# Three quarters of w_out loaded ahead of batch 1, the first batch's second layer cut 12 to 4, 36 fillers in small groups: one change to a fused attention and MoE kernel on one core

## The chip, the core and the metric

The kernel runs on one core of one Trainium2 chip. Five engines work side by side, each through its own queue in program order: PE (TensorE, matrix products and transposes), ACT (ScalarE), DVE (VectorE), POOL (GpSimd) and SP (SyncE, here only an issuer of transfers). Transfers between HBM and on-chip memory run on 16 DMA engines; SP's and ACT's go through hardware queues, POOL's through a software queue. The metric is the device time of one execution in microseconds.

## The reference

Eight batches of linear attention with cosine weights, heads concatenated, feed a two-layer network whose gate is h cos(h).

```python
def phi(x, c, s):
    r = np.maximum(x, 0.0)
    return np.concatenate([r * c, r * s], axis=-1)
q_p = phi(q, cos_w, sin_w)
k_p = phi(k, cos_w, sin_w)
kv = np.einsum('bhsf,bhsd->bhfd', k_p, v)
z = np.sum(k_p, axis=2)
num = np.einsum('bhsf,bhfd->bhsd', q_p, kv)
den = np.einsum('bhsf,bhf->bhs', q_p, z)[..., None] + 1e-06
...
h = x @ w_in
g = h * np.cos(h)
return (g @ w_out).astype(np.float32)
```

q, k and v are 8 x 8 heads x 576 tokens x 64, in 32-bit floats; x has 4608 tokens of 512; w_in is 512 x 2048, w_out 2048 x 512.

## The kernel before

**Stages.** Tokens go through in chunks of 512: chunk b holds most of batch b, cut into four tiles of 128 tokens, and a fifth tile of each pair of batches gathers the rest for a ninth chunk. For each batch: `load` brings q, k and v to the raw buffers (one buffer per name, reused by every batch; two transfers each, one for each half of the partitions); `prep` (L364 to L369) multiplies max(x, 0) with a cosine or sine and rounds to 16 bits, once for each tile and each of the two functions g, on ACT or DVE; `cast_v` rounds V; `q_pe` (L428, copies at L435 and L437) transposes a tile of q on PE; `kv` (L397) sums k times v over all tiles, in two halves of four heads (copied out at L410 and L412, or L415); `num` (L464, then L481 to L485 on DVE) forms numerators and denominators of a tile and divides; `x_pe` (L519, L524) transposes the result. `layer1` (L575 for chunks 0 and 1) multiplies with w_in, and `gate` takes the cosine on ACT (L547) and the product on DVE (L549). `layer2_plain` (L878), for chunk 0 alone, multiplies with w_out; from chunk 1 on a form with sums of blocks is used (`layer2`, L953; the sums over w_out are made once on DVE, `w_out_sums`, L901).

**Order.** The program records about 1,400 steps in `Plan`. A step may have several engines to choose from. Two literal tables, `STARTS` and `ENGS`, give each step a number and an engine; `run` sorts the steps by that number and emits them, so the table is the order on each engine's queue. The numbers in it have no other use.

**The front.** PE starts with matmuls on a constant tile, here called fillers (`warm`, L1041): 28 ahead of q's transposes, 17 after the first of these, and 4, 3 and 2 between the numerators of batch 0. Their results aren't used.

**Weights.** They come through POOL's queue in quarters, and are held back by small copies on POOL that write one element of each quarter's destination, so that the transfer has to come after them. `weights` lets w_in's first half go when a given piece of q has been prepared (`HQ` = tile, function, number of hops: the copy reads it through as many small copies); `weights2` lets the second half go when a tile of V has been cast (`WS2`), then w_out's first `WQ` quarters when w_in's first has landed. `hold_raw` (L1098) does the same for batch 1's raw buffers: they wait for the quarter that `RAW1` names. `part_of_w_out` (L1115) lets the rest of w_out go when a piece of batch 1's q has landed. `layer2_plain` sums over hidden units in two parts, and the first takes as many of the sixteen blocks of 128 as `WQ` quarters hold; the first part's result is copied out by ACT (L886), the second's added by DVE (L889):

```python
WQ = OPT["WQ"] * NJT // 4
for jh, js in enumerate((range(WQ), range(WQ, NJT))):
    for n, t in enumerate(range(NT)):
```

```python
GATE1 = ((w_in_sb[0:2, 0, R1 * Dff // 4 + 1:R1 * Dff // 4 + 2], [("w_in", R1)]) if R1 < 4 else
         (w_out_sb[0:2, (R1 - 4) * NJT // 4, 1:2], [("w_out", R1 - 4)]))
```

Of the kernel before, what the change touches and what calls it, by code (L numbers as in the profile page):

```python
# [13 lines left out]
F16 = mybir.dt.float16  # L14
# [3 lines left out]
OPT = dict(F16=0, WS2=[3, 1], HQ=[1, 0, 1], AQ=0, W2F=0, WQ=2, L2F=0, WFI=None, XPE=[0, 1, 2, 3, 4], FAST1={3:  # L18
           2, 4: 2, 5: 2, 6: 4, 7: 4, 8: 4}, MODE={}, HH='', LD=[['k', 0], ['v', 0], ['q', 0], ['k', 1], ['v',
           1], ['q', 1]], NB=[['A0', 'A1'], ['A0', 'A1', 'M0']], XB=[['B3'], ['B3', 'M1']], W0=5, W1=6,  # L20
           WF=[[2, 2, 2, 2], [2, 2, 0, 0]], HOLD=['k', 1], P0=0, RAW1=2, WO2=1, H1=0, DA=0, W2=0, SQ=0, NUZ=1)
# [1440 lines left out]
```

## Time and profile before

| | |
|---|---|
| device time, median of 3 runs | 281.50 us (281.26 to 281.94) |
| the profiled execution | 281.42 us, span 279.6 us |
| granted clock of PE | 1.00 |
| HBM read, written | 36.75 MB, 11.80 MB |

The span runs from the first to the last recorded instruction; 1.8 us of the execution's time lie around it. Rows of the timeline give start and length in us, engine, line, operation and what is written from what; in brackets stands the idle time before, and what ended it. The chain of waits is followed back from the last instruction; its rows are start, length, engine, tile and line. Rows of transfers end with the median time from issue to landing, and rows of DMA queues give packets, MB and share of the 16 engines' time.

### The profile page before, as it was taken

Reading aid. Unit: us, or ns where it says so; the run is one execution under the profiler, and the core shown is the slowest. Engines: PE = TensorE matmul, PEld = TensorE weight load, DVE = VectorE, ACT = ScalarE, POOL = GpSimd, SP = SyncE. Lnnn points to the kernel's source line nnn. Section 1 sums busy time; section 2 is a strip of 40 time slices with the busy share of each in tenths; the row PEclk is TensorE's granted clock in tenths of the full one; section 3 lists DMA queues with packets and bytes.
Section 4 is the critical chain, followed back from the end, with each engine's and each line's share of the span. In section 5 each row is a group of like instructions: output and inputs, shape, how many; then the busy total and the mean of one; then the engine's idle time right before and its main releaser. Section 6 shows DMA issues by size and latency. Waiting matters only on the chain.

```text
span 279.6 us, 6829 instructions
## 1 busy us (share of the span) xinstructions
PE 272.5 (97%) x2698; PEld 215.5 (77%) x2698; DVE 236.4 (85%) x442; ACT 210.0 (75%) x363; POOL 83.4 (30%) x104
## 2 busy tenths in 40 slices
PE   8999999999999999999999999999999999999993
PEld 2567867787966677769776878789988888888882
DVE  1767698989999999999999998989989879873952
ACT  2756699879998897788989978995758696776330
POOL 1340020030502101520440045132534372399210
PEclk9999999999999999999999999999999999999999
DMA  6999999989999999969999998739756495697125
GB/s 209 337 205 205 361 218 258 338 282 181 324 303 263 242 230 264 285 200 287 216 249 265 212 260 283 109 104 142 161 76 146 102 159 102 150 146 123 75 77 150
DMA packets 80223, 58.03 MB, mean 208 GB/s; under 512 B 43200, under 2 KB 77248, under 8 KB 80192
## 3 DMA queue, kind: packets, MB, share of 16 engines
q1 hardware_dynamic: 68960, 39.99, 59.3%
q0 software_dynamic: 10496, 17.04, 29.3%
q10 hardware_dynamic: 736, 0.57, 0.7%
q8 instruction: 21, 0.34, 0.5%
q14 instruction: 10, 0.08, 0.1%
HBM read 36.75 MB, written 11.80 MB: 174 GB/s over the span
## 4 chain that ended last, share of the span: by engine, by line
PE 92%; ACT 3%; DVE 2%; issue 1%; POOL 0%; ACTq 0%; POOLq 0%
PE M L953 34%; PE M L736 14%; PE M L608 11%; PE M L575 9%; PE TR L736 6%; PE ATT L1041 5%; PE ATT L464 3%; PE M L878 3%; PE ATT L397 3%; PE TR L608 2%; ACT KQ L368 1%; DVE XN L485 1%; PE M L428 1%; ACT V L382 0%; ACT ch L547 0%
## 5 line engine op out<-in xcount | busy, mean ns | idle before, releaser
L953 PEld LDWEIGHTS <-gT 128*128 128x128 f16 x560 | 53.9, 98 | 8.3
L953 PE MATMUL M<-w_out_sb,gT 128*128 128x256 f16 x448 | 57.1, 273 | 0.0
L549 DVE TENSOR_TENSOR gT<-M,ch 128x512 f16<-128x512 f32 x73 | 48.5, 684 | 5.9 <-ACT ch L547 5.7
L547 ACT ACTIVATE ch<-M 128x512 f32<-128x512 f32 x75 | 43.4, 596 | 12.2 <-PE M L575 5.4
L368 ACT ACTIVATE KQ<-km,CS 128x512 f16<-128x512 f32 x57 | 38.5, 718 | 1.6 <-DMA km<-in_k_dram 1.6
L964 ACT ACTIVATE ost<-M 128x512 f32<-128x512 f32 x41 | 24.3, 596 | 18.0 <-PE M L953 13.0
L368 ACT ACTIVATE KQ<-qm,CS 128x512 f16<-128x512 f32 x46 | 31.5, 721 | 4.0 <-DMA qm<-in_q_dram 4.0
L608 PE MATMUL M<-xT,w_in_sb 128*128 128x512 f16 x136 | 33.8, 379 | 0.0
L953 PE MATMUL M<-T,S 128*128 128x256 f16 x256 | 32.3, 273 | 0.0
L384 POOL CAST V<-vm 128x1024 f16<-128x1024 f32 (+1 forms) x18 | 15.8, 904 | 51.6 <-DVE den L481 21.6
L736 PEld LDWEIGHTS <-w_in_sb 128*128 128x128 f16 x288 | 27.3, 98 | 4.8 <-issue 0.3
L575 PE MATMUL M<-xT,w_in_sb 128*128 128x256 f16 x256 | 30.3, 273 | 0.3 <-DVE gT L549 0.3
L953 PEld LDWEIGHTS <-S 128*128 128x128 f16 x256 | 24.8, 98 | 4.1 <-DVE S L929 0.2
L575 PEld LDWEIGHTS <-w_in_sb 128*128 128x128 f16 x256 | 24.4, 98 | 3.9 <-issue 0.5
L748 DVE TENSOR_TENSOR Z<-M,Z 128x512 f32<-128x512 f32 x31 | 21.1, 687 | 4.3 <-PE M L736 3.2
L608 PEld LDWEIGHTS <-w_in_sb 128*128 128x128 f16 x160 | 14.9, 98 | 12.2
L549 POOL TENSOR_TENSOR gT<-Z,ch 128x512 f16<-128x512 f32 x5 | 6.3, 1268 | 56.6 <-ACT ch L547 20.0
L485 DVE TENSOR_TENSOR XN<-ATT,rec 128x512 f16<-128x512 f32 x32 | 22.1, 692 | 1.1
L464 PEld LDWEIGHTS <-qT 128*128 128x128 f16 (+1 forms) x320 | 14.8, 101 | 5.6 <-issue 3.5
L759 ACT ACTIVATE ch<-Z 128x1024 f32<-128x1024 f32 x12 | 12.7, 1057 | 6.9 <-DVE Z L748 4.9
L744 ACT ACTIVATE Z<-M 128x512 f32<-128x512 f32 x26 | 15.2, 596 | 3.4 <-PE M L736 2.4
L464 PE MATMUL ATT<-kvz,qT 128*128 128x65 f16 (+1 forms) x288 | 16.0, 195 | 0.8 <-DVE XN L485 0.5
(152 smaller groups left out, 519.3 us busy)
## 6 DMA issues: line engine op xcount, KB each, us to landing
out_dram<-ost POOLq DMA_DIRECT2D x38, 256.0 KB, 4.1
qm<-in_q_dram SPq DMA_DIRECT2D x8, 640.0 KB, 6.3
km<-in_k_dram SPq DMA_DIRECT2D x8, 640.0 KB, 7.1
qm<-in_q_dram SPq DMA_DIRECT2D x8, 512.0 KB, 5.7
km<-in_k_dram SPq DMA_DIRECT2D x8, 512.0 KB, 5.9
vm<-in_v_dram SPq DMA_DIRECT2D x6, 640.0 KB, 6.0
vm<-in_v_dram SPq DMA_DIRECT2D x6, 512.0 KB, 4.4
w_in_sb<-in_moe_w_in_dram POOLq DMA_DIRECT2D x4, 512.0 KB, 7.5
```

The lines of the kernel that those rows point to most:

```text
L368: fn = {"ACT": lambda: nc.scalar.activation(out=out_, in_=in_, func=AF.Relu, scale=sc), "DVE": lambda: nc.vector.tensor_scalar(out=out_, i ...
L384: "POOL": lambda: nc.gpsimd.tensor_copy(out=out_, in_=in_)}
L464: nc.tensor.matmul(bank[hb][ps, hh * D1:(hh + 1) * D1], lhsT=x[:, h, :], rhs=z[:, h, :], start=True, stop=True)
L485: nc.vector.tensor_tensor(out=split(x16[n][:, hs, :], k), in0=A[:, :, :, 0:D], in1=split(rec[n][:, hs], k).unsqueeze(3).broadcast_to((P, k ...
L547: act(0.5, due, lambda: nc.scalar.activation(out=ch[c], in_=bank, func=AF.Sin, bias=math.pi / 2.0, scale=1.0), [key], [("ch", c)])
L549: mul(due, 0.61, lambda q: q.tensor_tensor(out=dst, in0=bank if len(dst.shape) == 2 else bank.rearrange("p (j s) -> p j s", j=dst.shape[1] ...
L575: nc.tensor.matmul(M1[m][:, jj * 2 * P:(jj + 1) * 2 * P], lhsT=w_in_sb[:, cc, j * P:(j + 1) * P], rhs=X[:, cc, ts], start=(cc == 0), stop= ...
L608: nc.tensor.matmul(M, lhsT=w_in_sb[:, cc, j * P:(j + 1) * P], rhs=X[:, cc, :], start=(cc == 0), stop=(cc == NCT - 1))
L736: nc.tensor.matmul(bank[0][:, j * TH:(j + 1) * TH], lhsT=a(cc, j), rhs=b[:, cc, :], start=(first and j == 0 and cc == 0), stop=(last and j ...
L748: dve(0.61, due + 0.3, lambda: nc.vector.tensor_tensor(out=dst, in0=bank[0], in1=dst, op=ALU.add), [bank[1], key], [key])
L953: nc.tensor.matmul(bank[0][:, tt * MH:(tt + 1) * MH], lhsT=a[:, j, tt * P:(tt + 1) * P], rhs=b[:, j, :], start=(first and (apart or tt == ...
L964: act(0.5, due, lambda: nc.scalar.activation(out=dst, in_=view(bank), func=AF.Copy), [bank[1]], dk)
```

## The change

- `WQ` from 2 to 3: three quarters of w_out are asked for ahead of batch 1, one after; the first part of chunk 0's second layer sums 12 blocks, the second 4.
- `RAW1` from 2 to 4: batch 1's raw buffers wait for w_out's first quarter in place of w_in's third.
- `W2F` from 0 to 2: the release of w_out's last quarter reads a single element of q's first part, through one more small copy.
- `HQ` from tile 1 to tile 3: w_in's first half is let go by another tile of q.
- `FW`, new: the fillers ahead of batch 0's kv are 20, 4, 4, 4 and 4 (36) in place of 28 and 17 (45), as steps of their own, so that the table can put other steps between them.
- The tables are new. On PE they put the transposes of q's tiles 1, 0 and 3 after the first 20 fillers, then 4 fillers, tile 2's transposes, 12 fillers and kv; the copies of tiles 0 and 1 come ahead of k's preparations on DVE and ACT; batch 0's numerators begin with tile 0. For batch 1, three groups of 12 matmuls with w_out stand ahead of its first transposes, and DVE's first sum over w_out stands ahead of its norms. Batch 2's preparations of k are spread among batch 1's copies. One preparation of batch 2's k, one of batch 3's k and one of batch 3's q go from DVE to ACT. From about the second chunk's second layer on the order is the same on PE.

```diff
-OPT = dict(F16=0, WS2=[3, 1], HQ=[1, 0, 1], AQ=0, W2F=0, WQ=2, L2F=0, WFI=None, XPE=[0, 1, 2, 3, 4], FAST1={3:
...
+OPT = dict(F16=0, WS2=[3, 1], HQ=[3, 0, 1], AQ=0, FW=[20, 4, 4, 4, 4], W2F=2, WQ=3, L2F=0, WFI=None, XPE=[0,
...
-           WF=[[2, 2, 2, 2], [2, 2, 0, 0]], HOLD=['k', 1], P0=0, RAW1=2, WO2=1, H1=0, DA=0, W2=0, SQ=0, NUZ=1)
+           'M1']], W0=5, W1=6, WF=[[2, 2, 2, 2], [2, 2, 0, 0]], HOLD=['k', 1], P0=0, RAW1=4, WO2=1, H1=0,
+           DA=0, W2=0, SQ=0, NUZ=1)
...
-        warm(28, 9.05)
+        if OPT["FW"]:
+            for i, n in enumerate(OPT["FW"]):
+                warm(n, 7.5 if i == 0 else 0.2157 * n)
+        else:
+            warm(28, 9.05)
...
-        warm(17, 3.67, rd=[("TR", 0)])
+        if not OPT["FW"]:
+            warm(17, 3.67, rd=[("TR", 0)])
```

The rest of the diff is the tables.

More of the change, by code (lines that the diff above doesn't have):

```diff
@@ L15 @@
 SYNC = mybir.DependencyInfo(mybir.DependencyClass.Sync, mybir.DependencyReason.DATA)
-OPT = dict(F16=0, WS2=[3, 1], HQ=[1, 0, 1], AQ=0, W2F=0, WQ=2, L2F=0, WFI=None, XPE=[0, 1, 2, 3, 4], FAST1={3:
-           2, 4: 2, 5: 2, 6: 4, 7: 4, 8: 4}, MODE={}, HH='', LD=[['k', 0], ['v', 0], ['q', 0], ['k', 1], ['v',
-           1], ['q', 1]], NB=[['A0', 'A1'], ['A0', 'A1', 'M0']], XB=[['B3'], ['B3', 'M1']], W0=5, W1=6,
-           WF=[[2, 2, 2, 2], [2, 2, 0, 0]], HOLD=['k', 1], P0=0, RAW1=2, WO2=1, H1=0, DA=0, W2=0, SQ=0, NUZ=1)
@@ L24 @@
-STARTS = (
[98 rows of a table removed]
+OPT = dict(F16=0, WS2=[3, 1], HQ=[3, 0, 1], AQ=0, FW=[20, 4, 4, 4, 4], W2F=2, WQ=3, L2F=0, WFI=None, XPE=[0,
+           1, 2, 3, 4], FAST1={3: 2, 4: 2, 5: 2, 6: 4, 7: 4, 8: 4}, MODE={}, HH='', LD=[['k', 0], ['v', 0],
+           ['q', 0], ['k', 1], ['v', 1], ['q', 1]], NB=[['A0', 'A1'], ['A0', 'A1', 'M0']], XB=[['B3'], ['B3',
+           'M1']], W0=5, W1=6, WF=[[2, 2, 2, 2], [2, 2, 0, 0]], HOLD=['k', 1], P0=0, RAW1=4, WO2=1, H1=0,
+           DA=0, W2=0, SQ=0, NUZ=1)
+STARTS = (
[98 rows of a table added]
 )
@@ L124 @@
 ENGS = (
-    "DDPSSSSSSSSDAPDDDPADAPDDAPAGGGGPDADADDDADADADADDADADGGGGGGPPADPPDPPAPPDPPAPPDPPAPPDPAPAD"
-    "PADPADPADPADPADPADPADPADPADPADPADPADPADPADPADGSSGSSGGGGGSSSSDADADADADADAPDDAPADAPDDAPADA"
-    "DADADDADADPPAPPDPAPPDPAPPDPAPPDPAPDPPDPAPAPAPAPAPDPDGGPDPDGGPADPADPADPADPADPADPADPADPADP"
-    "ADPADPADPADPADPADPADDDDDSSSSSSADADAADDAAGGGPPADASDDSAASAASPPDPAPPDPAPPDPAPPDPADDDPPAPPDD"
-    "PPAPPAPPDPPDGGPPAGGPADPADPADPADPADPADPADPADPADPADPADPADPADPADPADPADSSSSSSDDAAAAAAAAGGGPP"
-    "ADASAASDASAASADPPDSPPDSPPDSPPDSSPPDSDDDDDDDPPAPPDDPPAPPAPPDPPDGGPPAGGDDDDPAPDAGPAPAPDPDA"
@@ L131 @@
-    "DPADPADPADPADPADPAPDAGPAPAPDPDADPADPADPADPADPADSSSSSSAAAAAADAAAGGGPPAAASAASAASADSPPDSPPD"
-    "SPPDSPPDSDDDPPAPPDDPPAPPAPPDPPDGGPPAGGDDDDPAPDAGPAPAPDPDADPADPADPADPADPADPAPDADPAPAPDPDA"
-    "DPADPADPADPADPADSSSSSSDDAAAAAAADGGGPPAADSAASDDSAASAAPPDSPPDSPPDSPPDSSPPDSDDDPPAPPADPPAGG"
-    "PPAPPAPPAGGPPAGGGGDDDDPAPDAGPAPAPDPDADPADPADPADPADPADPAPDADPAPAPDPDAGPADPADPADPADPADSSSS"
-    "SSAAAAAAADAAGGGPPAAASADSADSAASPPDSPPDSPPDSPPDSDDDDDDDPPAPPADPPAGGPPAPPAPPAGGPPAGGGGDDDDP"
-    "APDADPAPAPDPDADPADPAPDAGPAPAPDPDAGPADPAPDADPAPAPDPDADPADPAPDADPAPAPDPDADPADSSSSSSDAAAAAA"
@@ L137 @@
-    "AAAGGGPPADASDASAASDDSAAPPDSPPDSPPDSPPDSSPPDSDDSPPAPPAGGPPAGGPPAPPAPPAGGPPAGGGGDDDDPAPDAG"
-    "PAPAPDPDAGPADPAPDADPAPAPDPDADPADPAPDADPAPAPDPDADPADPAPDADPAPAPDPDADPADDDDDSPPAPPDGGPPAPP"
-    "APPDPPDGGPPAGGDDDDPAPDAGPAPAPDPDAGPADPAPDAGPAPAPDPDAGPADPAPDAGPAPAPDPDADPADPAPDAGPAPAPDP"
-    "DADPADDDDDDDPPAPPDDDPPAPPAPPDPPDSASAAPPDSADSA"
+    "DDPPPPPSSSSSSSSDAPDDDPADAPDDAPAGGGGDADADDDADADADADDADADGGGGGGGPPADPPDPPAPPDPPAPPDPPAPPDP"
+    "APADPADPADPADPADPADPADPADPADPADPADPADPADPADPADPADGSSGSSGGGGGSSSSDADADADADADAPDDAPADAPDDA"
@@ new lines @@
+    "PADADADADDADADPPAPPDPAPPDPAPPDPAPPDPAPDPPDPAPAPAPAPAPDPDGGPDPDGGPADPADPADPADPADPADPADPAD"
+    "PADPADPADPADPADPADPADPADDDDDSSSSSSDAAAAAADDAGGGPPAADSDDSAASAASPPDPAPPDPAPPDPAPPDPADDDPPA"
+    "PPDDPPAPPAPPDPPDGGPPAGGPADPADPADPADPADPADPADPADPADPADPADPADPADPADPADPADSSSSSSAAADAAAAAAG"
+    "GGPPAAASAASDASAASADPPDSPPDSPPDSPPDSSPPDSDDDDDDDPPAPPDDPPAPPAPPDPPDGGPPAGGDDDDPAPDAGPAPAP"
+    "DPDADPADPADPADPADPADPAPDAGPAPAPDPDADPADPADPADPADPADSSSSSSAAAAAADAAAGGGPPAAASAASAASADSPPD"
+    "SPPDSPPDSPPDSDDDPPAPPDDPPAPPAPPDPPDGGPPAGGDDDDPAPDAGPAPAPDPDADPADPADPADPADPADPAPDADPAPAP"
@@ new lines @@
+    "DPDADPADPADPADPADPADSSSSSSDDAAAAAAADGGGPPAADSAASDDSAASAAPPDSPPDSPPDSPPDSSPPDSDDDPPAPPADP"
+    "PAGGPPAPPAPPAGGPPAGGGGDDDDPAPDAGPAPAPDPDADPADPADPADPADPADPAPDADPAPAPDPDAGPADPADPADPADPAD"
+    "SSSSSSAAAAAAADAAGGGPPAAASADSADSAASPPDSPPDSPPDSPPDSDDDDDDDPPAPPADPPAGGPPAPPAPPAGGPPAGGGGD"
+    "DDDPAPDADPAPAPDPDADPADPAPDAGPAPAPDPDAGPADPAPDADPAPAPDPDADPADPAPDADPAPAPDPDADPADSSSSSSDAA"
+    "AAAAAAAGGGPPADASDASAASDDSAAPPDSPPDSPPDSPPDSSPPDSDDSPPAPPAGGPPAGGPPAPPAPPAGGPPAGGGGDDDDPA"
+    "PDAGPAPAPDPDAGPADPAPDADPAPAPDPDADPADPAPDADPAPAPDPDADPADPAPDADPAPAPDPDADPADDDDDSPPAPPDGGP"
@@ L141 @@
+    "PAPPAPPDPPDGGPPAGGDDDDPAPDAGPAPAPDPDAGPADPAPDAGPAPAPDPDAGPADPAPDAGPAPAPDPDADPADPAPDAGPAP"
+    "APDPDADPADDDDDDDPPAPPDDDPPAPPAPPDPPDSASAAPPDSADSA"
 )
```

196 rows, old and new, of the table STARTS are left out of this document.

## The prediction

> **What bounds the kernel now.** I read the busy line and the chain of the page first, then busy time in 10 us windows.
>
> ```profile
> PE 272.5 (97%) x2698; PEld 215.5 (77%) x2698; DVE 236.4 (85%) x442; ACT 210.0 (75%) x363; POOL 83.4 (30%) x104
> PE 92%; ACT 3%; DVE 2%; issue 1%; POOL 0%; ACTq 0%; POOLq 0%
> 34.00:44.00 10.00, 9.99 (x109) 6.74 (x107) 9.72 (x23) 9.72 (x19) 2.08 (x3) 1.00 0.96 217
> 44.00:54.00 10.00, 9.77 (x104) 6.69 (x103) 8.97 (x24) 8.31 (x16) 0.00 (x0) 1.00 1.09 332
> 54.00:64.00 10.00, 10.00 (x123) 7.75 (x122) 9.21 (x19) 8.26 (x16) 2.60 (x3) 1.00 0.93 281
> 64.00:74.00 10.00, 10.00 (x116) 8.75 (x114) 9.11 (x19) 9.89 (x18) 3.67 (x5) 1.00 1.04 218
> 74.00:84.00 10.00, 10.00 (x110) 7.39 (x108) 9.79 (x16) 9.69 (x18) 1.08 (x3) 1.00 1.10 322
> ```
>
> After the stretch and its length, the columns are PE, PEld, DVE, ACT, POOL. PE is full from 34 us on, and the chain is PE for 92% of the span. What the change can win is therefore either matmuls that aren't needed (filler) or time in which PE waits. Both lie at the front, so I followed the chain through the first 45 us:
>
> ```profile
> 1.32 8.94 PE ATT L1041 x28
> 10.26 0.45 PE TR L428 x8
> 11.15 3.67 PE ATT L1041 x17
> 15.27 1.22 PE M L397 x40
> 16.52 0.44 DVE kvz L412
> 23.13 0.61 DVE gT L549
> 23.78 10.72 PE M L575 x96
> 35.02 1.60 ACT KQ L368 x3
> 37.33 0.59 ACT ch L547
> 43.59 0.60 ACT kvz L415
> 44.23 0.29 PE ATT L464 x4
> ```
>
> Two stretches aren't real matmul work. Up to 23.78 it is filler and waits for DVE; from 34.5 to 44.2 the chain runs over ACT, which prepares batch 1, while PE stays just busy enough beside it (9.99 of 10). The second stretch starts from transfers, so I asked for the DMA issues and queues:
>
> ```profile
> w_out_sb<-in_moe_w_out_dram POOLq DMA_DIRECT2D x1, 512.0 KB, 10.3
> km<-in_k_dram SPq DMA_DIRECT2D x1, 640.0 KB, 7.7
> vm<-in_v_dram SPq DMA_DIRECT2D x1, 320.0 KB, 7.6
> q0 software_dynamic: 195, 0.20, 119.8%
> q1 hardware_dynamic: 5, 0.01, 1.7%
> q0 software_dynamic: 26, 0.03, 34.6%
> q0 software_dynamic: 138, 0.14, 100.3%
> 16.96 1.48 POOL L1093 DMA_DIRECT2D w_out_sb<-in_moe_w_out_dram  x2 [0.30 <-POOL w_out_sb L1083]
> 24.78 0.18 POOL L1098 CAST km<-w_in_sb 2x1 f32<-2x1 f16 x1 [6.33 <-DVE gT L549]
> 25.70 0.60 SPq L336 DMA_DIRECT2D km<-in_k_dram  x1
> 32.17 0.62 SPq L336 DMA_DIRECT2D vm<-in_v_dram  x1
> 37.28 1.90 POOL L1093 DMA_DIRECT2D w_out_sb<-in_moe_w_out_dram  x2 [0.30 <-POOL w_out_sb L1115]
> 42.09 0.60 SPq L339 DMA_DIRECT2D km<-in_k_dram  x1
> ```
>
> Rows four and five are the queues of GpSimd (q0) and SP (q1) from 27 to 28 us: batch 1's k is asked for from about 25 on (release at 24.78), yet its queue moves next to nothing until the weights before it are through. The queues serve one after the other, and a quarter of a weight (0.52 MB written) at 0.20 to 0.21 MB per us takes 2.55 us. So w_out's first quarter lands at 16.96 + 10.3 = 27.3, k1's last part at 25.70 + 7.7 = 33.4, v1's last at 32.17 + 7.6 = 39.8.
>
> **The change, part by part.** *Filler: 45 become 36 ahead of batch 0's kv.* The row of 17 gives 0.216 us each, so nine are 1.94 us; the first group ends 8 x 0.216 = 1.73 earlier, at 8.53. Whether PE can use it is read from DVE and ACT:
>
> ```profile
> 7.15 2.07 DVE L369 TENSOR_SCALAR KQ<-qm,CS 128x512 f16<-128x512 f32 x5 [5.17 <-DMA qm<-in_q_dram]
> 10.71 1.95 ACT L368 ACTIVATE KQ<-km,CS 128x512 f16<-128x512 f32 x3 [1.64 <-DMA km<-in_k_dram]
> 13.97 0.70 DVE L383 CAST V<-vm 128x256 f16<-128x256 f32 x3
> 13.96 0.72 ACT L382 ACTIVATE V<-vm 128x256 f16<-128x256 f32 x2
> 14.58 0.68 DVE L437 COPY qT<-M 128x1024 f16<-128x1024 f16 x1
> 17.57 0.22 DVE L481 TENSOR_SCALAR den<-M 128x4 f32<-128x4 f32 x2
> 20.84 0.17 DVE L481 TENSOR_SCALAR den<-ATT 128x8 f32<-128x8 f32 x1 [0.98 <-PE ATT L464]
> 21.10 1.03 PE L575 MATMUL M<-xT,w_in_sb 128*128 128x256 f16 x8
> 42.58 1.02 ACT L435 ACTIVATE qT<-M 128x1024 f16<-128x1024 f16 x1
> ```
>
> q's tile 1 is prepared at about 8.4, tiles 0 and 3 at 8.8 and 9.2 (five in 2.07 us). The transposes (0.45 each) run at 8.53, 8.98, 9.43; four fillers, tile 2's transposes and twelve fillers end at 13.79. The copies of tiles 1 and 0 (1.02 on ACT, 0.68 on DVE) fall before 10.71, where both engines now stand and wait for k: they cost nothing, and would cost 0.68 to 1.02 if k landed before about 10.2. From 10.71 both engines have the same k and V work as now, so V's last casts end at 14.68 as now, and kv's second half starts at 14.75 and ends 0.61 later, at 15.36, against 16.49 now. DVE must then do tile 2's copy first (to about 15.4) and kvz's second half (0.44), so the numerators start near 16.0 instead of 17.0.
>
> *The order of the norms.* Now four of them take DVE from 17.57 to 23.13 with 0.98 of waiting, 4.58 of work. With tile 0 first and the attention bank free in time, they run from 16.43 to about 20.95. Tile 1's x is transposed at 18.8; from its transposes to the first layer-1 matmul I take 1.07 as now, giving 19.9 instead of 21.10. The third group needs its bank freed by the first group's gate (cosine 0.59 on ACT, product 0.61 on DVE, and the steps between, 1.6 after the group's last matmul): 19.9 + 0.87 + 1.6 = 22.4 against 23.78, where DVE came from the norms only at 23.13. The fourth needs a second gate on ACT, between x's copies, which takes some 0.2 back. I take **1.2 us** won when layer 1 runs steadily; the ends are 0.4 (only kv's earlier start counts) and 1.94 (every filler).
>
> *HQ, tile 3 for tile 1* (w_in's release): both are the last of q's five DVE preparations, so w_in leaves at the same time: 0. POOL's copy that releases w_out (done before 16.96) reads w_in's first quarter, so that is there 3 us before 19.9: cover enough; a later POOL would cost what exceeds it.
>
> *Three quarters of w_out, batch 1's loads released by w_out's first quarter.* SP's order is unchanged; POOL gets one more issue ahead of the four releases. k1 is asked for 2.5 us later (27.4), and one more quarter lies before it, also 2.55: these overlap, so batch 1 lands 2.55 later, k1 at 36.0, v1 at 42.4. w_out's third quarter lands near 32.8. Layer 1's twelve steady groups (96 matmuls in 10.72) put w_out's first group at about 34.3 now and 33.1 then; its ninth matmul, the first to want that quarter, comes at 33.1 + 8 x 0.216 = 34.9: hidden, by 2 us.
>
> *12 to 4.* Three groups of twelve ahead of kv(1) instead of eight put 12 x 0.216 = 2.59 of w_out's matmuls before anything of batch 1 is needed; this covers the 2.55. ACT, the chain of this stage, copies out the first twelve's result at 35.9 and prepares k1 from 36.3. Now it needs 9.2 from its first k (35.02) to kvz's end (44.19); then it has one preparation of q more and that copy less, so kvz would end at 45.6, and with a wait for kv at 45.96: PE gets through three twelves (7.77), two groups of layer 1 (1.75), three sets of transposes (1.35) and kv (1.22) from 33.1 to 45.2. The numerators start at 46.0 instead of 44.23, 1.8 later, with 2.59 of matmuls and one set of transposes (0.45) more behind them. 2.59 + 0.45 - 1.8 = 1.2: the gain is carried, the stage itself is **0**. If its cover failed, up to 2.55 would be lost; if PE's present waits closed too, 0.3 won.
>
> *w_out's last quarter* waits for q's first part alone through a hop (two POOL copies of 0.2), and lands near 45 by its place behind v1. After it, DVE's first sum over w_out now stands ahead of batch 1's norms, at about 45.7: 0, unless the quarter is later.
>
> *Three preparations from DVE to ACT* (batch 2's k, batch 3's k and q): at 0.65 each (three in 1.95) 1.95 more for ACT. By the windows ACT has 1.69 + 1.74 + 0.11 + 0.31 = 3.85 us idle from 44 to 84. It starts 1.8 later, should end 1.2 earlier, and does one preparation before: 3.85 - 1.8 - 1.2 - 1.95 + 0.65 = -0.45. Nothing is left on paper; but preparations follow one another faster (42.58 to 43.59 holds a copy of 1.02, so ends overlap), and PE needs them only at kv(2) and kv(3). I take 0, with 0.4 to 1.2 as its price.
>
> The order of instructions after some 84 us is the same on PE, so nothing is added there. Sum: 281.42 (this execution; 0.08 under the median of 281.50) - 1.2 = **280.2 us**.
>
> [...] Here the rows above (27 to 28 us, and the seventh, 43 to 44 us, where batch 2's k had been asked for at 42.09) show one queue being emptied first. [...]
>
> **The rivals.** *ACT becomes the bound* between 45 and 84 us: for it speaks the -0.45, against it that ACT falls to 8.3 of 10 for 20 us. PE then waits for gates and x copies; 0.4 to 1.2 lost, 280.6 to 281.4, say 280.9. Chance 0.17.
>
> *DVE waits at w_out's sum.* If the last quarter shares the engines with k2, its transfer, from 40.8, ends at 45.0 instead of 43.4 and it lands near 46.6 instead of 45.0. DVE, in order, holds all of batch 1's norms for 0.95 us, and PE, which needs the fourth tile's x just in time, loses it: 281.2. The row of 43 to 44 us, all q0, speaks against. Chance 0.10.
>
> *Slower: batch 1 lands later than the twelve matmuls cover.* Its release now hangs on a transfer that lands 27.3; the kernel's queue behind a new issue needs about 2 us to its first byte (w_out's issue at 37.28 has moved 0.03 MB from 38 to 39.5, the sixth row). If k1 begins only after such a gap, or w_out's quarters are slower, k1's last part comes at 38 instead of 36, ACT's chain, which has no idle time there, moves with it, and kvz is at 48. From 36.3 on each us of k1 is one of the end: 280.2 + 2.0 = 282.2. Against it: the release leaves 3 us of weights still queued. Chance 0.14.
>
> **How the numbers follow.** Forecast 0.53, the rivals 0.17, 0.10, 0.14, and 0.06 for something not seen, half of it slow. 0.3% of 281.5 is 0.84 us, about what can be told from no change: faster is below 280.66. That takes nearly all of the forecast and a quarter of the first rival: faster 0.56, the same 0.28, slower 0.16. The likeliest case's own range is 279.5 (all nine fillers) to 280.9. For 8 in 10 it reaches to 279.3, as PE's present 0.24 wait may close too, and to 282.1, most of the slow rival.
>
> **What would show it.** Right: the first layer-1 matmul near 19.9 and steady ones 1.2 earlier; k1 preparations from 36.3; kv(1)'s second half near 44.6; the numerators of batch 1 at 46.0 without more than 0.4 us of PE idle; PE full after. Wrong: the first group of q's transposes not before 9; a PE gap above 1 us between 42 and 47, or ACT's first k after 37 (slow rival); DVE's first sum over w_out starting after 46 behind a DMA; ACT at 9.9 of 10 with PE idle between 50 and 80. If the front gains 1.2 but the end doesn't, the sum's step "the gain is carried" is the one that fails.

## The result, and the profile after

The changed kernel takes 285.13 us in the median (283.83 to 286.31, 6 runs) against 281.40 (281.01 to 281.94, 6 runs) of the kernel before beside it: a ratio of 1.0134, interval 1.0113 to 1.0154. A second series gave 284.11 (283.9 to 284.75) and 1.0081 (1.0057 to 1.0104). Slower by about 1%, and outside the range 279.3 to 282.1. The profiled execution is the fastest one of the first series: 283.83 us, span 282.0. In the changed kernel lines stand one to six further down (L464 is L465, L886 is L887).

The page after, first the busy time of each engine, then the chain of waits:

```profile
PE 271.3 (96%) x2689; PEld 214.3 (76%) x2689; DVE 235.6 (84%) x439; ACT 211.6 (75%) x366; POOL 83.6 (30%) x105
...
PE 73%; DMA 13%; ACT 7%; DVE 2%; issue 2%; SPq 1%; DVEq 0%; ACTq 0%
```

PE has 1.2 us less to do and the kernel takes 2.4 longer in these two profiles. The chain, PE for 92% before, now runs through transfers for 13% and through ACT for 7%. The windows that were shown of before, columns as there (PE, PEld, DVE, ACT, POOL, clock, share of DMA, GB/s), say where:

```profile
34.00:44.00 10.00, 10.00 (x85) 6.15 (x84) 7.23 (x19) 8.27 (x17) 1.50 (x3) 1.00 1.12 314
44.00:54.00 10.00, 8.52 (x114) 5.78 (x111) 7.88 (x24) 8.02 (x15) 0.00 (x0) 1.00 1.01 343
54.00:64.00 10.00, 10.00 (x134) 8.56 (x133) 9.43 (x18) 9.73 (x18) 2.60 (x3) 1.00 0.45 140
64.00:74.00 10.00, 8.91 (x97) 7.48 (x96) 8.38 (x19) 8.96 (x17) 1.42 (x2) 1.00 1.12 223
74.00:84.00 10.00, 9.92 (x116) 7.37 (x115) 9.43 (x15) 9.35 (x18) 3.33 (x6) 1.00 1.12 339
```

PE misses 1.48 from 44 to 54 and 1.09 from 64 to 74; from 54 to 64 the transfers, at 0.93 before, are down to 0.45. The timeline of the changed kernel has the front first (start, length, engine, line; in brackets the idle time and its releaser):

```profile
7.48 2.07 DVE L370 TENSOR_SCALAR KQ<-qm,CS 128x512 f16<-128x512 f32 x5 [5.51 <-DMA qm<-in_q_dram]
...
8.81 1.09 PE L429 MATMUL M<-IDENT,KQ 128*128 128x128 f16 x16 [0.98 <-DVE KQ L370]
...
19.78 1.03 PE L576 MATMUL M<-xT,w_in_sb 128*128 128x256 f16 x8
...
45.86 0.29 PE L465 MATMUL ATT<-kvz,qT 128*128 128x65 f16 x4 [0.24 <-ACT kvz L416]
```

Up to here it is as forecast: first layer-1 matmul at 19.78 (19.9 was said), batch 1's numerators at 45.86 (46.0). Against before that is 1.63 later, with 3.04 of PE work less behind, by the prediction's count: 1.4 us ahead. (Against a second profile of before, and counted from q's first preparation, it is 0.75; the table below has both.) The next 25 us lose it:

```profile
49.51 0.72 ACT L369 ACTIVATE KQ<-km,CS 128x512 f16<-128x512 f32 x1 [1.70 <-DMA km<-in_k_dram]
50.14 0.58 ACT L887 ACTIVATE ost<-M 128x512 f32<-128x512 f32 x1
...
50.77 1.04 PE L879 MATMUL M<-w_out_sb,gT 128*128 128x512 f16 x4 [1.17 <-ACT ost L887]
...
57.08 0.72 ACT L369 ACTIVATE KQ<-km,CS 128x512 f16<-128x512 f32 x1
...
57.82 0.60 SPq L340 DMA_DIRECT2D km<-in_k_dram  x1
58.48 0.63 SPq L337 DMA_DIRECT2D km<-in_k_dram  x1
59.20 0.60 SPq L337 DMA_DIRECT2D vm<-in_v_dram  x1
59.90 8.29 SPq L442 DMA_TRANSPOSE qT<-KQ  x3
...
68.66 0.43 PE L465 MATMUL ATT<-kvz,qT 128*128 128x65 f16 x8 [1.08 <-DMA qT<-KQ]
```

Two things are to be seen. ACT stands 1.70 us for batch 2's k, at the head of its queue, and the copy of w_out's third result, which PE needs for a free bank, stands behind it: PE waits 1.17. Then batch 2's preparations of k last until 57.8, batch 3's k is asked for only then, and the transposes of batch 2's q queue behind it: PE waits 1.08 for the first of them, at batch 2's numerators. The same transposes and the same numerators before:

```profile
55.52 0.60 SPq L339 DMA_DIRECT2D km<-in_k_dram  x1
56.51 0.60 SPq L336 DMA_DIRECT2D km<-in_k_dram  x1
58.20 0.60 SPq L336 DMA_DIRECT2D vm<-in_v_dram  x1
59.73 6.03 SPq L441 DMA_TRANSPOSE qT<-KQ  x3
...
67.34 0.42 PE L464 MATMUL ATT<-kvz,qT 128*128 128x65 f16 x8
```

The list of DMA issues gives the first transpose's time from issue to landing, before:

```profile
qT<-KQ SPq DMA_TRANSPOSE x1, 5.9
```

and after:

```profile
qT<-KQ SPq DMA_TRANSPOSE x1, 8.7
```

It landed at 59.73 + 5.9 = 65.6 before, 1.7 us before PE wanted it; now it is issued 0.2 later and lands at 59.90 + 8.7 = 68.6, the moment at which PE goes on.

### The profile page after: what moved, and what is told of

The parts are those of the page before. It is cut to its first block, busy times and chain, and to the rows that moved or that the text cites. A ratio compares the mean times of both kernels' runs of the same rounds, so it can differ in the third digit from the quotient of the medians.

```text
span 282.0 us, 6820 instructions
## 1 busy us (share of the span) xinstructions
PE 271.3 (96%) x2689; PEld 214.3 (76%) x2689; DVE 235.6 (84%) x439; ACT 211.6 (75%) x366; POOL 83.6 (30%) x105
## 4 chain that ended last, share of the span: by engine, by line
PE 73%; DMA 13%; ACT 7%; DVE 2%; issue 2%; SPq 1%; DVEq 0%; ACTq 0%
PE M L954 30%; PE M L737 14%; PE M L576 7%; PE M L609 6%; PE TR L737 6%; DMA qT<-KQ 5%; DMA qm<-in_q_dram 4%; ACT KQ L369 4%; DMA km<-in_k_dram 3%; PE ATT L465 2%; ACT ch L548 2%; PE M L879 2%; PE ATT L398 2%; PE TR L609 2%; PE ATT L1042 1%
## 5 line engine op out<-in xcount | busy, mean ns | idle before, releaser
L954 PEld LDWEIGHTS <-gT 128*128 128x128 f16 x560 | 53.8, 98 | 8.1
L369 ACT ACTIVATE KQ<-km,CS 128x512 f16<-128x512 f32 x59 | 40.2, 719 | 1.9 <-DMA km<-in_k_dram 1.7
L369 ACT ACTIVATE KQ<-qm,CS 128x512 f16<-128x512 f32 x47 | 32.4, 723 | 4.8 <-DMA qm<-in_q_dram 4.4
L550 POOL TENSOR_TENSOR gT<-Z,ch 128x512 f16<-128x512 f32 x5 | 6.3, 1267 | 56.5 <-ACT ch L548 20.0
L465 PEld LDWEIGHTS <-qT 128*128 128x128 f16 (+1 forms) x320 | 14.7, 101 | 7.9 <-issue 3.1
L465 PE MATMUL ATT<-kvz,qT 128*128 128x65 f16 (+1 forms) x288 | 16.0, 195 | 2.2 <-DMA qT<-KQ 1.5
```

Of the source, the lines that this page charges most:

```text
L369: fn = {"ACT": lambda: nc.scalar.activation(out=out_, in_=in_, func=AF.Relu, scale=sc), "DVE": lambda: nc.vector.tensor_scalar(out=out_, i ...
L465: nc.tensor.matmul(bank[hb][ps, hh * D1:(hh + 1) * D1], lhsT=x[:, h, :], rhs=z[:, h, :], start=True, stop=True)
L550: mul(due, 0.61, lambda q: q.tensor_tensor(out=dst, in0=bank if len(dst.shape) == 2 else bank.rearrange("p (j s) -> p j s", j=dst.shape[1] ...
L954: nc.tensor.matmul(bank[0][:, tt * MH:(tt + 1) * MH], lhsT=a[:, j, tt * P:(tt + 1) * P], rhs=b[:, j, :], start=(first and (apart or tt == ...
```

## The experiments

Their tables of numbers were made by moving steps of one table to places of the other. Lines in most of them stand two further down than in the changed kernel (L465 is L467). T, R1, R2 and D are the theories: **T**, batch 2's preparations stand ahead of batch 1's copies; **R1**, three preparations more load ACT too much; **R2**, the later landing and the 12 to 4 cut are the root; **D**, which came after the second series, batch 2's transposes queue behind loads that are asked for too late.

### The front alone, and the rest alone

```diff
 the changed kernel's OPT, front and fillers; loads, order and engines from batch 1 on as before
-WQ=3, RAW1=4, W2F=2
+WQ=2, RAW1=2, W2F=0
```

> The front alone: 36 fillers in groups of 20, 4, 4, 4 and 4, q's transposes and copies in the new order, tile 0 first; all else (two quarters of w_out ahead of batch 1, eight and eight, the engines and the order from batch 1 on) as before. T (the loss comes from batch 2's preparations standing ahead of batch 1's copies): first layer-1 matmul at 19.8, batch 1's numerators about 1.3 earlier than before's 44.2, and the gain reaches the end: 280.1 (279.8 to 280.6). R1 (ACT overloaded by three preparations) and R2 (the 12 to 4 cut) expect the same. If it gives 281.4, the front's gain is lost behind batch 1's loads whatever stands there, and the cut is needed to keep it.

Measured: 281.55 (280.33 to 282.64, 12 runs), ratio 1.001 (0.9993 to 1.0026). The first layer-1 matmul came at 19.42 (19.8 was expected) and the best execution took 280.33, but the median shows no gain. None of the three theories expected that; it is the case of the expectation's last sentence. The chain of waits of that run comes to batch 1's numerators through the transfer of batch 1's q (start, length, engine, tile and line):

```profile
26.80 9.83 DMA qm<-in_q_dram
...
36.75 1.48 DVE KQ L372 x3
...
38.37 0.61 PE M L431 x8
```

In before's profiles that stretch of the chain has layer 1's matmuls and ACT, and no transfer.

```diff
 the changed kernel's loads, order and engines from batch 1 on; before's front
-HQ=[3, 0, 1], FW=[20, 4, 4, 4, 4]
+HQ=[1, 0, 1], FW=[]
```

> The rest alone: before's front (28 and 17 fillers, old order), then the changed kernel from there on. T: batch 2's k still lands at about 49.4, because its issue hangs on batch 1's k and not on PE; ACT and DVE stand until then as in the changed kernel, so the front's 1.3 us makes no difference: 283.8 to 284.3, and the idle time of ACT ahead of batch 2's first k falls by about 1.3. If gain and loss simply add up (R1, R2): the changed kernel's time plus 1.3, about 285.2 to 286.4.

Measured: 283.98 (282.39 to 284.25), ratio 1.0082 (1.0063 to 1.01). That is T's number: the old front with the new rest is no slower than the whole change. So the whole loss lies behind the front, and the front gives nothing there.

### Undoing the order and the engines of batch 2

```diff
 ACT's queue
-k of batch 2, tile 1 sine; copy of w_out's third result; k, tile 2 sine; copy of the fourth; x of tile 0
+copy of w_out's third result; copy of the fourth; x of tile 0; k of batch 2, tiles 1 and 2 sine
 DVE's queue
-k of batch 2, tile 3 sine; norms of batch 1's tiles 1 and 2
+norms of batch 1's tiles 1 and 2; k of batch 2, tile 3 sine
```

> The changed kernel with three steps moved in their own queues: ACT's first two preparations of batch 2's k behind the two copies of w_out's results and tile 0's x, DVE's first behind the norms of tiles 1 and 2. T: the copies no longer wait for the load; the step from 46 to 60 us gives back 1.2 to 1.4, and ACT, which then works in its 1.7 us of idle time, is ahead for batch 2's q as well (another 1.1): 1.2 to 2.5 under the changed kernel, 281.3 to 282.6 for its fast executions. R1: ACT is full from 50 to 70 us anyway: at most 0.4 back. R2: nothing back.

Measured: 284.04 (282.91 to 284.86), ratio 1.0093 (1.0075 to 1.0111), no better than the changed kernel's second series. PE's wait for the copy was gone, and batch 2's numerators came at 69.09 behind the transposes all the same, 60.80 after q's first preparation against 61.18 in the changed kernel. T's first loss is real; taking it away alone wins 0.4 at that point, and nothing in the median.

```diff
 engines in the table
-batch 2 k tile 0 sine, batch 3 k tile 0 cosine, batch 3 q tile 0 cosine: ACT
+batch 2 k tile 0 sine, batch 3 k tile 0 cosine, batch 3 q tile 0 cosine: DVE
```

> The changed kernel with three preparations back on DVE (batch 2's k tile 0 sine, batch 3's k and q tile 0 cosine), order as it is. R1: 1.95 us less for ACT where it stands at 10.0 of 10, so batch 2's transposes come 1.1 earlier and more: 1.1 to 2.0 under the changed kernel. T: the stall at 47.8 to 49.5 stays with its 1.4; of the late transposes at most part comes back: 0 to 0.8 under it. R2: 0.

Measured: 284.89 (282.56 to 286.33), ratio 1.0117 (1.0083 to 1.015): nothing back.

Then the changed kernel again, and larger parts of the old order put back:

> The changed kernel once more, as the measure for the runs beside it. 283.8 to 286.3, median near 285, as before. If q's first landing sets the spread (theory of the front: 20 fillers end before q is prepared, so the front moves with the load), the first layer-1 matmul of the profile stands 12.3 after the first preparation of q, as in the earlier profile (7.46 and 19.78).

Measured: 284.11, as told above; q's first preparation at 7.84, first layer-1 matmul at 20.14, so 12.30 behind it.

```diff
 all ten preparations of batch 2's k, and the load of batch 3's k
-ahead of and among batch 1's copies of x
+behind batch 1's copies of x, on the engines they had before
```

> The changed kernel with one thing undone: batch 2's ten preparations of k stand where they stood before the change, behind the copies of x and the first two cosines, on the engines they had, with the load of batch 3's k behind them as before. T (the place of these preparations): ACT and DVE no longer stand for the load at 47.8 to 49.5, the preparations follow one another and end near 56 instead of 57.7, batch 3's k is asked for near 55.5 instead of 57.8, the transfers' idle time at 54 to 59 shrinks, and batch 2's q comes in time: 2.0 to 3.0 under the changed kernel, 282 to 283 in the median. R1 (ACT's load): one preparation less on ACT, 0.4 to 0.7. R2 (the 12 to 4 cut): 0.

Measured: 285.50 (284.9 to 287.95), ratio 1.015 (1.0112 to 1.0188). **T falls here**: its place undone, the kernel is slower than the change beside it. In the timeline of that run PE is busy to 59.8 us, waits 0.55 for a gate, and then, at batch 2's numerators, for the transposes:

```profile
54.08 0.71 ACT L371 ACTIVATE KQ<-km,CS 128x512 f16<-128x512 f32 x1
...
57.76 1.32 ACT L371 ACTIVATE KQ<-km,CS 128x512 f16<-128x512 f32 x2
...
69.89 0.43 PE L467 MATMUL ATT<-kvz,qT 128*128 128x65 f16 x8 [2.06 <-DMA qT<-KQ]
```

The preparations of k begin on ACT at 54.08 (52.71 in before's first profile) and end at 59.1, not at 56: batch 1's copies and cosines hold ACT until then. The new order had worked against that, and the wait for the transposes doubles without it.

```diff
 all preparations, casts, loads and transposes of batches 2 to 7
-the changed kernel's places and engines
+before's places and engines
```

> As the run beside it, and all preparations, casts, loads and transposes of batches 2 to 7 in their old places and on their old engines; of the change there remain the front, the three quarters of w_out, and 12 to 4. T: the rest of the loss goes with batch 2's k, so this is within 0.5 of the run beside it, 281.5 to 283. R1: the step from batch 2's k alone to this one is the large one, over 1. R2: it stays above 283.5.

Measured: 285.54 (285.01 to 286.73), ratio 1.0135 (1.0108 to 1.0163): as its neighbour, so the places and engines of these steps behind batch 2 do not show in the time.

### The transposes

```diff
 SP's queue
 load k of batch 3, both parts
-load v of batch 3, first part
 transposes of batch 2's q, tiles 0 to 2
+load v of batch 3, first part
```

> The changed kernel with one load moved on SP's queue: the first part of batch 3's v goes behind the first three transposes of batch 2's q instead of ahead of them. D (the loss sits in batch 2's transposes, which queue behind the loads of batch 3 that were asked for too late): the first transposes land 1.7 us earlier or more (0.64 MB at 0.36 MB per us), PE's wait of 1.1 to 1.5 at batch 2's numerators goes, and 0.8 to 1.5 comes back against the changed kernel: 282.6 to 283.9. R1 (ACT's load sets the pace from 50 to 70): nothing, 284 to 285.

Measured: 282.71 (281.87 to 284.59, 11 runs), ratio 1.004 (1.0016 to 1.0063). One load moved gives back 1.4 us against the changed kernel's second series, 2.4 against its first (ratios 1.0081 and 1.0134, each to before's runs beside it). The first transpose of that run now lands in

```profile
qT<-KQ SPq DMA_TRANSPOSE x1, 4.9
```

and its timeline has batch 2's numerators without a wait:

```profile
59.95 5.40 SPq L444 DMA_TRANSPOSE qT<-KQ  x3
...
67.58 0.42 PE L467 MATMUL ATT<-kvz,qT 128*128 128x65 f16 x8
...
73.77 0.49 PE L578 MATMUL M<-xT,w_in_sb 128*128 128x256 f16 x3 [0.67 <-DVE gT L552]
```

**D holds.** The last row is new: PE waits 0.67 for a gate.

> The same, and batch 2's first three preparations of k moved behind batch 1's copies as in the earlier run of that name. D: alone that move gained nothing that the late transposes did not take again; with the transposes out of the way its 1.2 shows, so 1.0 to 2.5 under the changed kernel and under the run beside it by 0.5 or more: 281.8 to 283. R1: as the changed kernel.

The edit is that of the run before and the two queues of ACT and DVE from the third experiment. Measured: 282.32 (281.4 to 283.16, 12 runs), ratio 1.0026 (1.0007 to 1.0045), 1.8 under the changed kernel's second series, as D expected, but only 0.4 under its neighbour. Its timeline has batch 2's numerators at 66.87 (68.66 in the changed kernel), and then the next wait opens:

```profile
71.92 0.62 POOL L387 CAST V<-vm 128x512 f16<-128x512 f32 x1 [15.64 <-DMA vm<-in_v_dram]
...
72.57 0.48 DVE L372 TENSOR_SCALAR KQ<-km,CS 128x512 f16<-128x512 f32 x1 [1.81 <-POOL V L387]
...
73.71 1.03 PE L578 MATMUL M<-xT,w_in_sb 128*128 128x256 f16 x8 [1.31 <-DVE gT L552]
```

Batch 3's v, now behind the transposes, is late for its cast on POOL; DVE's next preparation has to follow that cast (`run`'s caller puts such steps of DVE and POOL in one sequence), the gate stands behind it, and PE waits 1.31.

```diff
 SP's queue, against the run above
-load v of batch 3, first part, behind the transposes of tiles 0 to 2
+load v of batch 3, first part, behind the transpose of tile 0 alone
```

> The changed kernel with batch 2's first three preparations behind batch 1's copies, and the first part of batch 3's v behind the first transpose alone instead of behind three. D: the first transpose has only batch 3's k ahead of it, and v comes 3 to 4 us sooner than behind three, so the idle time at 72 to 74 (1.31) goes: 281.2 to 282.0 against 282.3 behind three. If the second transpose is the one that counts, it waits for v again: 282.5 to 283.5.

Measured: 282.59 (281.25 to 283.31, 12 runs), ratio 1.0038 (1.0017 to 1.0058). PE's wait at 73 was gone in the profile, but the median is no better. The number is that of the second expectation, its cause isn't: no transpose was waited for. In the two profiled executions it did turn into time (batch 2's to batch 7's numerators are 0.84 us nearer, table below). Why the medians don't show it stays open.

> The run beside it and three preparations back on DVE (batch 2's k tile 0 sine, batch 3's k and q tile 0 cosine). R1 (ACT's load): 0.5 to 1.5 under the run beside it. Otherwise (ACT's load costs nothing by itself): within 0.4 of it.

The edit is the run above with the three preparations on DVE. Measured: 283.45 (282.27 to 284.83, 10 runs), ratio 1.0073 (1.0048 to 1.0098): 0.9 slower than the run above by the medians, though the intervals overlap. **R1 falls**: with the three preparations off ACT the kernel is no faster, and rather slower.

### The loads, and the cut

```diff
 layer2_plain of the changed kernel
-        WQ = OPT["WQ"] * NJT // 4
+        WQ = NJT // 2
```

> The changed kernel, all loads as they are, with w_out's matmuls cut 8 to 8 again. PE has 2.59 us of matmuls less ahead of batch 1's kv and as much more behind. If the cover ahead of kv only moves PE's idle time (batch 1 and 2 come when ACT, DVE and the transfers are ready, in both), this takes the same time, 283.5 to 285, with 1.5 to 2.6 of idle time ahead of kv and none at batch 2's numerators. If 12 to 4 is worth its 2.59, it is slower by 1 or more.

Measured: 287.73 (285.76 to 288.1, 5 runs), ratio 1.0203 (1.0169 to 1.0236). By the medians the cover is worth 2.6 to 3.6 us against the changed kernel's two series; the fastest executions of the two kernels differ by 1.9. The prediction's term for the cut, 2.59, is right in size as far as these tell.

```diff
 the changed kernel
-RAW1=4
+RAW1=2
```

> The changed kernel with batch 1's loads released by w_in's third quarter again, so asked for 2.5 us earlier (25 instead of 27.4), and the three quarters of w_out ahead of them as they are. If the queue of the weights is emptied first, batch 1's k lands at 36 as it does now and the time is the changed kernel's within 0.5 (284 to 285). If the engines take turns between the queues, k lands up to 2.5 earlier and w_out's third quarter later, and the time falls by 1 or more.

Measured: 284.93 (283.83 to 286.22, 4 runs), ratio 1.0115 (1.008 to 1.015): as the changed kernel. Batch 1's k was asked for at 25.71 and 26.43 instead of 27.44 and 28.16, and its two parts took this long to land (list of issues, the second part first):

```profile
km<-in_k_dram SPq DMA_DIRECT2D x1, 640.0 KB, 10.7
km<-in_k_dram SPq DMA_DIRECT2D x1, 512.0 KB, 9.7
```

against 7.7 and 6.6 in the changed kernel: asked for earlier by 1.7, they wait longer by 3 and land some 1.3 later. The queues of GpSimd (q0, w_out) and SP (q1, batch 1) in that run, from 30 to 31 us:

```profile
q0 software_dynamic: 121, 0.12, 72.1%
q1 hardware_dynamic: 122, 0.12, 44.9%
```

Each moved 0.12 MB, so neither was emptied first. In the changed kernel the same microsecond has 0.20 MB on q0 and 0.01 on q1. The prediction's "the queues serve one after the other" holds for the rows that it read and not for these. Why k lands later here, and not as early as in the changed kernel or earlier, stays open.

```diff
 the front alone (first experiment), w_out's matmuls 8 to 8, order and engines as before
-WQ=2, RAW1=2, W2F=0
+WQ=3, RAW1=4, W2F=2
```

> The front alone, the old order and engines, w_out's matmuls cut 8 to 8; only the loads are those of the changed kernel: three quarters of w_out ahead of batch 1, which so lands 2.5 us later. If the later landing is the root: PE idle 2 to 2.6 us more by batch 1's kv and something at batch 2's numerators, 283.8 to 285.5. If the new order is the root: 281.5 to 282.

Measured: 283.43 (282.46 to 285.2, 7 runs), ratio 1.0076 (1.0048 to 1.0104). The later landing by itself costs 1.9 us against the front alone, a little under what R2 expected. In its profile PE loses it in one place, and nothing at batch 2's numerators:

```profile
36.64 0.48 DVE L372 TENSOR_SCALAR KQ<-km,CS 128x512 f16<-128x512 f32 x1 [2.97 <-DMA km<-in_k_dram]
...
38.38 1.03 PE L578 MATMUL M<-xT,w_in_sb 128*128 128x256 f16 x8 [2.59 <-DVE gT L552]
```

### The front, once more

> The front alone, once more, for a second profile: its times spread from 280.3 to 282.6 where before's lie within 0.9. If the front's spread comes from q's first landing alone, its first layer-1 matmul stands 12.3 after the first preparation of q, and the time differs from the earlier 280.33 by the difference of the landings (7.08 there). If it differs by more, the rest is lost later, where transfers are waited for.

Measured: 282.19; q's first preparation at 7.65, first layer-1 matmul at 19.95. The landing explains 0.54 of the 1.86 by which it is over the other profile; of the rest, 0.6 is a wait for a transpose ahead of batch 4's numerators, at 107 us.

```diff
 SP's queue of the front alone
-load v of batch 3, first part; transpose of batch 2's q, tile 0
+transpose of batch 2's q, tile 0; load v of batch 3, first part
```

> The front alone, with the first part of batch 3's v behind the first transpose of batch 2's q on SP's queue. D: what its median loses against its best (281.55 against 280.33) is partly late transposes (0.6 of 0.95 in the second profile stood at batch 4's, none at batch 2's in the first), so a few tenths come back: 280.8 to 281.4. If the front's spread comes from q's first landing and from layer 1's waits alone: 281.5 as without.

Measured: 282.64 (281.19 to 284.36, 12 runs), ratio 1.0037 (1.0011 to 1.0064). Neither expectation has that number: it is 1.1 over the front alone (ratio 1.001), so the load moved wins nothing where those transposes aren't late, and may cost. The profiled execution, the fastest, shows no wait of PE for v or for a transpose; where the others lose is not known.

> The kernel before, once more, for a second profile. In the first one its first layer-1 matmul stands 13.95 after the first preparation of q (7.15 and 21.10), and its clock rose late (the first 28 fillers took 8.94); the new front has 12.30 in every profile. If the 13.95 is that one execution's, this one has 12.6 to 13.3 and the front is worth 0.3 to 1.0, not 1.2 to 1.6.

Measured: 280.59, and its timeline:

```profile
1.31 8.08 PE L1041 MATMUL ATT<-S 128*128 128x512 f16 x28 [1.31 <-POOL S L1023]
...
20.23 1.03 PE L575 MATMUL M<-xT,w_in_sb 128*128 128x256 f16 x8
```

The same 28 fillers took 8.94 in the profile of the prediction, whose first row of the granted clock starts at 6.87 us (5.46 in the changed kernel's). In this one the first layer-1 matmul stands 12.98 after q's first preparation at 7.25, not 13.95.

```diff
-        warm(28, 9.05)
+        warm(19, 9.05)
```

> The kernel before with nine fillers fewer in its first group (28 to 19), nothing else. If fillers are what the front gains, as forecast in part, the first layer-1 matmul comes 0.4 to 1.2 sooner and the time falls by 0.3 to 1.0: 280.4 to 281.1. If V's casts and the norms set it: 12.6 to 13.3 after q's first preparation as in the run beside it, and 281.2 to 281.7.

Measured: 281.07 (280.38 to 281.65, 12 runs), ratio 0.9992 (0.9975 to 1.0009): no change. Its first layer-1 matmul came at 19.97, 12.76 after q, within the second expectation; the median lies at the upper edge of the first.

### All profiles, counted from q's first preparation

The start of q's first preparation on DVE (a), the first layer-1 matmul (b), and the first numerators of batch 1 (c), batch 2 (d) and batch 7 (e), from the timelines, in us; differences from them:

| kernel | a | b - a | c - a | d - c | e - d | time of that execution |
|---|---|---|---|---|---|---|
| before, first profile | 7.15 | 13.95 | 37.08 | 23.11 | 124.55 | 281.42 |
| before, second profile | 7.25 | 12.98 | 36.09 | 23.11 | 124.55 | 280.59 |
| before, nine fillers less | 7.21 | 12.76 | 36.03 | 23.31 | 125.13 | 281.26 |
| front alone | 7.11 | 12.31 | 35.94 | 23.11 | 124.56 | 280.33 |
| front alone, second profile | 7.65 | 12.30 | 36.33 | 23.10 | 125.53 | 282.19 |
| front alone, v behind one transpose | 7.66 | 12.29 | 36.27 | 23.10 | 124.55 | 281.19 |
| late landing, 8 to 8, old order | 7.57 | 12.30 | 38.59 | 23.11 | 124.55 | 283.33 |
| the rest alone, before's front | 7.64 | 12.77 | 38.91 | 22.48 | 124.55 | 283.32 |
| changed | 7.48 | 12.30 | 38.38 | 22.80 | 125.52 | 283.83 |
| changed, second profile | 7.84 | 12.30 | 38.38 | 22.89 | 125.94 | 284.75 |
| changed, copies and norms first | 8.29 | 12.30 | 38.89 | 21.91 | 125.60 | 284.39 |
| changed, three preparations on DVE | 7.51 | 12.29 | 38.38 | 22.64 | 126.91 | 284.97 |
| changed, 8 to 8 | 7.64 | 12.29 | 37.97 | 24.58 | 125.85 | 285.76 |
| changed, batch 1 released by w_in | 7.68 | 12.30 | 38.77 | 23.18 | 125.74 | 285.03 |
| changed, batch 2's k in its old place | 7.43 | 12.30 | 38.38 | 24.08 | 126.08 | 285.50 |
| changed, batches 2 to 7 in their old places | 7.82 | 12.31 | 38.69 | 23.54 | 125.40 | 285.01 |
| changed, v behind three transposes | 7.75 | 12.29 | 38.51 | 21.32 | 125.58 | 282.81 |
| the same, and copies first | 7.56 | 12.30 | 38.60 | 20.71 | 126.23 | 282.75 |
| v behind one transpose, copies first | 7.79 | 12.29 | 38.59 | 20.75 | 125.39 | 282.11 |
| the same, three preparations on DVE | 7.46 | 12.29 | 38.38 | 20.74 | 126.76 | 282.94 |

d - c is 23.11 wherever PE only works there with 8 to 8. With 12 to 4 it should be 23.11 - 3.04 = 20.07 by the prediction's count; the least that was reached is 20.71. e - d is 124.55 wherever PE only works. The rest alone reaches that with the new loads and the new order, and two runs with the old ones miss it (125.13 and 125.53).

## Why the prediction was wrong, point by point

- **Filler and norms, "1.2 us won when layer 1 runs steadily".** 21.10 became 19.78, so the forecast of 19.9 was right; its reference was not. 21.10 came from an execution in which the fillers took 0.86 longer than in the next. From q's first preparation the old front takes 13.95, 12.98 and 12.77 in three profiles (the last one, 7.64 and 20.41, is that of the rest alone), the new one 12.30 in all: the term is 0.5 to 0.7, not 1.2.
- **"The gain is carried": the step that failed**, in two ways. First, with the old loads there was little room to carry it. In before's two profiles batch 1's numerators follow the first layer-1 matmul by 23.13 and 23.11 us (c - b), so PE and ACT were the bound there, as the prediction read it. But the transfers stand close behind: for b - a of 12.98, 12.76, 12.31 and 12.30, c - a is 36.09, 36.03, 35.94 and 36.33. Of the 0.67 by which the front alone beats before's second profile, 0.15 is left at batch 1's numerators, and its chain runs through the transfer of batch 1's q. That fits its ratio of 1.001. Second, with the new loads what PE is ahead by at 46 us (0.75, counted from q) is waited away behind.
- **Batch 1 2.55 later, three groups of twelve as its cover.** Right in size: k1's last part landed at 28.16 + 7.7 = 35.9 (36.0 was said), the late landing costs 1.9 alone (the run with 8 to 8 and the old order), and the cover gives 2.6 to 3.6 by the medians (8 to 8 in the changed kernel). c - a grows by 2.3, which is the 3.04 of work put ahead less the 0.75 that is won; PE is busy for 25.68 of the 26.08 us from the first layer-1 matmul to these numerators. But it covers PE at batch 1 only. Batch 1's norms on DVE and its copies on ACT end some 4 us later (53.8 and 55.0, against 49.8 and 51.2 before). Later too are the end of batch 2's preparations of k (57.8, and 56.5 before), the request for batch 3's k (57.82, 55.52), and the landing of batch 2's first transpose (68.6, 65.6). PE, with 3.04 of work less between, arrives there 1.08 too early. d - c is 22.80 instead of 20.07: 2.73 lost, of which 1.17 stands at the copy and 1.08 at the transposes. No run comes under 20.71, so up to 0.6 of the 2.73 may be the count's.
- **Batch 2's k spread among batch 1's copies** had no term in the sum at all. It costs 1.17 at the head of ACT's queue, and saves more: undone, d - c rises to 24.08.
- **"The order of instructions after some 84 us is the same on PE, so nothing is added there."** e - d is 0.97 and 1.39 longer in the changed kernel's two profiles. The order on PE says nothing of the transfers beside it: at 93.83 and 108.78 PE waits for transposes again (0.18 and 0.20 by the rows; the rest of the 0.97 is in gaps too short to be named). But the rest alone, with the same loads and order, has 124.55, and the front alone, with the old ones, once 125.53: that this part of the loss comes from the change is not shown.
- **Three preparations to ACT, 0.** Right in sign at least: ACT runs at 9.73 and 10.00 of 10 from 50 to 70 us while PE waits, which is one of the signs of being wrong that the prediction named, but with the preparations back on DVE the kernel is 0.9 slower once the transposes are in time, and no faster before.
- **w_out's last quarter, 0**: DVE's first sum started at 45.62 (45.7 was said). **HQ, 0**: w_out's first group on PE at 32.94 (33.1). The rivals on w_out's sum and on a late batch 1 did not happen.

The changed kernel against the second profile of before, from q's first preparation to batch 7's numerators: 186.70 - 183.75 = 2.95, made of +2.29 up to batch 1's numerators (3.04 of work put ahead, 0.75 won), -0.31 between batches 1 and 2 (3.04 of work less, 2.73 lost), +0.97 behind.

No version was faster than the kernel before; the best with the new loads has 1.0026, the fillers alone 0.9992. What stays open: what makes the 0.97 behind batch 2's numerators, why the wait at 73 us, gone with v behind one transpose, gave no time in the median, and what of the spread of the new front's times (280.33 to 282.64) beyond q's landing and batch 4's transposes is in the executions that were not profiled.

## What to carry to other kernels

A full engine can be the bound by a hair only: move the start of its work, and see how far the next thing that depends on a load moves with it. Here 0.67 at the front was 0.15 at the next batch's numerators. Twelve matmuls pulled forward covered a load that came 2.5 us later, but only for the batch they stood ahead of; where each load waits for the buffer of the one before, a delay is handed from batch to batch (batch 3's k was asked for at 57.82, and at 55.52 before), and it has to be followed to the transfer on which the busy engine waits next. And a term read off one execution should be read from a mark that moves with the load (q's first preparation), since 0.9 of 1.3 us here belonged to that execution.

## What the runs showed of the hardware

- The same 28 fillers took 8.94 and 8.08 us in two executions of the kernel before. In the first of them a filler's record is 0.63 us long up to the one that starts at 5.99 us, 0.61 at 6.41, 0.40 at 6.84 and 0.38 from 7.08 on. In the changed kernel it is 0.63 up to 4.71, 0.55 at 5.13 and 0.38 from 5.52 on. The trace's first row of the granted clock, at 1.00, starts at 6.87 us in the one and at 5.46 in the other; ahead of it there is no row, and the windows read 1.00 there as well. Why it starts later in the one than in the other is not shown.
- q's first preparation started between 7.11 and 8.29 us, though SP issued its first loads at 0.74 and 1.55 us in before's first profile (7.15) and at 0.74 and 1.56 in the changed kernel's (7.48). With the new front, whose first 20 fillers end before q's first tile is prepared (PE waits 0.98 for it in the changed kernel), the first layer-1 matmul moves with it (12.3 us behind in every profile).
- The same transpose took 8.7 us from issue to landing with 640 KB of v asked for just ahead of it on SP's queue, and 4.9 with that load behind it.
- The two queues of weights and of batch 1 moved 0.12 MB each from 30 to 31 us where batch 1's loads were released earlier, and 0.20 and 0.01 MB in the changed kernel.
